# Linear-attention and token-mixer block, fp32 on one core: one transpose for the 64 leftover channels of two token tiles

## The chip, the cores and the metric

The kernel runs on one core of a Trainium2 chip. The metric is the device time of one execution in microseconds (us), lower is better. The kernel before has a median of 438.84 us over 3 runs (438.82 to 439.01).

## What is computed

x holds 2048 tokens of 448 channels. Six modulation vectors come from a condition vector; a modulated layer norm feeds a linear attention with 16 heads of 28 channels, and a second modulated layer norm feeds an MLP that mixes tokens. Everything is fp32. Cut to what matters here:

```
mod = (_silu(c) @ w_mod).reshape(c.shape[0], 6, 1, -1)
h = _layernorm(x, axis=-1) * (1 + ca) + sa
qkv = h @ wqkv
phi = lambda t: jnp.where(t > 0, t + 1, jnp.exp(t)) + 1e-6
pq, pk = phi(q), phi(k)
kv = jnp.einsum("bhsd,bhse->bhde", pk, v)
z = jnp.einsum("bhsd->bhd", pk)
o = einsum("bhqd,bhde->bhqe", pq, kv) / (einsum("bhqd,bhd->bhq", pq, z) + 1e-6)
x = x + ga * (o @ wo)
h = _layernorm(x, axis=-1) * (1 + cb) + sb
u = _gelu(jnp.einsum("bsd,sf->bdf", h, w1) + b1)
x = x + gb * (jnp.einsum("bdf,fs->bds", u, w2) + b2)
```

## The kernel before

**Numbers.** A product of fp32 matrices is made of a high and a low part of each operand (`hi` is the value rounded by a ScalarE copy, `lo` what VectorE subtracts), as hi·hi + hi·lo + lo·hi, each a TensorE matmul with a 128x128 stationary operand and up to 448 moving columns.

**Tiles.** The tokens are 16 tiles of 128. The 448 channels are contracted as three chunks of 128 and a rest of 64 (chunk 3). A tile must be transposed to bring channels onto partitions: four 128x128 TensorE transposes into the four quarters of one PSUM bank. To fill chunk 3, the 64 columns are first copied beside themselves (`a_dup`, L342, ScalarE; `b_dup`, L802, VectorE), so that after the transpose the same 64 channels stand in partitions 0–63 and 64–127. The weights of chunk 3 hold their high part in the upper 64 partitions and their low part in the lower 64. Chunk 3 then takes two matmuls (high and low part of the data) where chunks 0–2 take three each: 11 matmuls for one product.

**Order.** The program fixes each engine's order by hand: what is issued first runs first on its engine. In the profile an instruction is named by its output and inputs, such as `tp<-ident,h`.

**Phase A** (to about 105 us) goes over tiles, with tiles 0 to 2 written out. In step t of the loop over t=3..15 (L619–678) TensorE does `project` for k of tile t (`kp`, L381, 11 matmuls), the transposes of tile t+1 (`tp`, L350), and for tile t−3 `a_outer` (L478, 11 matmuls), which accumulates phi(k)ᵀh in four banks `cacc`: for each chunk high·high, low·high (phi(k)'s low part `pkl`) and, for chunks 0–2, high·low. ScalarE and VectorE split the transposed tile (`a_split`: `hh` on ScalarE L81, `hl` on VectorE L82, both 512 wide), normalise tile t+2 on VectorE (`a_norm_a` L332, `a_norm_b` L338), take exp and relu of kp (`a_exp`, ScalarE), add them to phi(k) (`pk`, VectorE L394), and split phi(k) and h. The q projections (`qp`) of most tiles come later.

**Phase B** (from about 115 us on; loop over i=0..20, L912–977) takes phi(q), already summed (`pq`), multiplies by the normalised reciprocal of the denominator (`b_scale`: `pn`, L699), duplicates the 64 columns (`b_dup`), transposes (`b_transpose`: `tq`, L809), splits (`b_high`: `pth`, ScalarE L814; `b_low`: `ptl`, VectorE L817), multiplies with the folded output weights `oh`/`ol` (`b_out`: `op`, L829, 11 matmuls), adds the residual (`b_res`: `x`, L838) and does the second layer norm in steps spread over three iterations: `b_norm1_a` (`y`, L848), `b_norm1_b` (`y`, L852, needs `rt` of the iteration before), `b_mean2` (GpSimd `ny`, ScalarE `sqb` L310), `b_norm2` (GpSimd `nb`, ScalarE `y` L870 and `h2h`), `b_low2` (`h2l`, VectorE L876). In iteration i TensorE does tq(i), op(i−1), one q projection while any are left, and from i=5 on 12 matmuls (`up`, L879–881) of the first MLP product for tile i−5. VectorE in iteration i does x(i−2), `b_prod` (`pd`, L685) for i+1, y(i−3), `b_sum` and `den` for i+1, y(i−3) again, ptl(i), pn(i+1), the duplicate of i+1, h2l(i−4), and a phi(q) sum where a q projection was made. The folded weights reach their rows by DMAs on SyncE's queue (`wp_rows`, L785–794).

The rest (both MLP products, the second by seven half-size products in the manner of Strassen) is not touched.

Of the kernel before, what the change touches and what calls it, by code (L numbers as in the profile page):

```python
# [36 lines left out]
QS = {0: 2, 4: 2}  # L37
SPLIT_AT = (8, 8, 9, 10, 11, 12, 12, 13, 13, 14, 14, 15, 15, 16, 17, 18)
# [5 lines left out]
NSLOT, NTOK = 76, 25  # L44
# [5 lines left out]
def block_kernel(ctx: ExitStack, tc: tile.TileContext, x, wqkv, wo, w1, b1, w2, b2, c, wmod, out):  # L50
# [170 lines left out]
    def w_low(j, ch):  # L221
        w, r = Whi[j, ch], raw_w[j, ch]
        if ch < 3:
            Wlo[j, ch] = moving(tslot, f"wl{j}_{ch}")
            nc.vector.tensor_sub(Wlo[j, ch], r, w.bitcast(F32))
        else:
            nc.vector.tensor_sub(w[64:128], r[64:128], w[64:128].bitcast(F32))

    def w_low_dma(j, ch):
        w, r = Whi[j, ch], raw_w[j, ch]  # L230
        if ch < 3:
            Wlo[j, ch] = moving(tslot, f"wl{j}_{ch}")
            lo, hi = Wlo[j, ch], w
        else:
            lo = hi = w[64:128]
            r = r[64:128]
        nc.scalar.activation(lo, hi.bitcast(F32), AF.Copy, scale=-1.0)
        nc.gpsimd.dma_start(lo, r, accum_op=ALU.add)
# [101 lines left out]

    def a_dup(t):
        nc.scalar.activation(hs[t][:, D:], hs[t][:, 384:D], AF.Copy)  # L342

    tps = {}

    def a_transpose(t):
        h = hs[t]
        tps[t] = bank(f"tp{t}")
        for ch in range(4):
            nc.tensor.transpose(tps[t][:, ch * P:(ch + 1) * P], h[:, ch * P:(ch + 1) * P], ident)  # L350

    def a_split(t):
        hh = slot(f"hh{t}", 512, F32R)
        hl = slot(f"hl{t}", 512, F32R)
        split(tps.pop(t), hh, hl)
        heads[t] = (hh, hl)

    def products(t, j, late):
# [3 lines left out]
        return [(hh, ch, Wlo[j, ch]) for ch in range(3)] + [(a, 3, Whi[j, 3]) for a in (hh, hl)]  # L362
# [5 lines left out]
    def project(t, j, name, late_low=False):  # L368
        hh, hl = heads[t]
        ps = bank(f"{name}{t}")  # L370
        o = ps[:, :D]
        todo = []
        for ch in range(4):
            a, b = (hh, ch, Whi[j, ch]), (hl, ch, Whi[j, ch])
            todo += [a, b] if ch == 3 else [a, (hh, ch, Wlo[j, ch]), b]
# [4 lines left out]
        for n, (a, ch, b) in enumerate(todo):  # L380
            nc.tensor.matmul(o, a[:, ch * P:(ch + 1) * P], b, start=(n == 0), stop=(n == 10))  # L381
# [87 lines left out]
    def a_outer(t):  # L469
# [4 lines left out]
        for ch in range(4):  # L474
            s = slice(ch * P, (ch + 1) * P)
            todo = [(xh, kh), (xh, kl)] + ([(xl, kh)] if ch < 3 else [])
            for i, (a, b) in enumerate(todo):
                nc.tensor.matmul(cacc[ch][:, :D], a[:, s], b, start=(t == 0 and i == 0),  # L478
                                 stop=(t == NT - 1 and i == len(todo) - 1))
# [76 lines left out]
    a_dup(1)  # L556
# [15 lines left out]
    a_dup(2)  # L572
# [13 lines left out]
    a_dup(3)  # L586
# [18 lines left out]
    a_dup(4)  # L605
# [13 lines left out]
    for t in range(3, NT):  # L619
        kp = project(t, 1, "kp")  # L620
        if t + 1 < NT:
            a_transpose(t + 1)
        a_outer(t - KV_LAG)
        if t in Q_EARLY:
# [3 lines left out]
        if t + 1 < NT:  # L628
            a_split(t + 1)
# [3 lines left out]
        for j, i in MOD_AT.get(t, ()):  # L633
            mod_part(j, i)
        if t == 14:
            fold(4)
        if 12 <= t < 16:
            nc.vector.tensor_mul(wo_sb[t - 12], wo_sb[t - 12], mods[2][:G])
        a_exp(t, kp)
        if t + 2 < NT:  # L640
            a_norm_b(t + 2)
        a_pk(t, kp)
        a_phi_q()
        a_pk_parts(t - 1)
# [138 lines left out]
    Wp_lo = [moving(tslot, f"ol{ch}") for ch in range(3)]  # L783

    def wp_rows(g, src, lows):  # L785
        r = g * G
        while r < (g + 1) * G:
            ch, at = divmod(r, P)
            n = min((g + 1) * G - r, P - at)
            if lows:  # L790
                dst = Wp_lo[ch][at:at + n] if ch < 3 else Wp_hi[3][64 + at:64 + at + n]
            else:
                dst = Wp_hi[ch][at:at + n]
# [477 lines left out]
```

## Time and profile before

| | before |
|---|---|
| median of 3 runs | 438.84 us |
| profiled execution, its own time | 439.32 us |
| span of the profile | 437.5 us |
| granted TensorE clock, mean | 0.999 |
| TensorE matmuls | busy 99% of the span, 2395 instructions |
| VectorE | busy 84%, 796 instructions |
| ScalarE | busy 62%, 576 instructions |
| GpSimd | busy 28%, 201 instructions |

The profiled execution has 1.8 us outside its span and lies 0.48 us above the median. A row of the timeline is the start in us, the duration, engine, line, operation, output and inputs with their shapes; in brackets stands how long the engine was idle before and who released it. The chain of waits is followed back from the last instruction of the program; PE is TensorE's matmul part, PEld its load of stationary operands, which runs a little ahead. On VectorE (DVE) the next instruction's start comes a little before the end of the one before it, so start-to-start distances, not durations, are what one instruction costs there.

### The profile page before, as it was taken

How to read it: one execution, taken by the hardware profiler on the slowest of the kernel's cores; microseconds unless marked ns; L12 is line 12 of the kernel's file. 1: busy time of each engine (PE TensorE's matmuls, PEld its weight loads, DVE VectorE, ACT ScalarE, POOL GpSimd, SP SyncE). 2: the span in 40 equal slices, each digit the busy share in tenths (PEclk: the TensorE clock that was granted, in tenths of full speed). 3: DMA queues.
4: the chain of work that ended last, by engine and by line, in shares of the span. 5: the costliest groups of instructions: out<-in, count | busy, mean ns of one | idle time of the engine just before them, and what ended most of it. 6: DMA issues, size and time to landing. Idle time of an engine off the chain costs nothing.

```text
span 437.5 us, 7310 instructions
## 1 busy us (share of the span) xinstructions
PE 432.9 (99%) x2395; PEld 403.1 (92%) x2395; DVE 367.0 (84%) x796; ACT 270.8 (62%) x576; POOL 123.3 (28%) x201
## 2 busy tenths in 40 slices
PE   8999999999999999999999999999999999999996
PEld 8699999999999999999999999999999999999996
DVE  5997898999898899996479487349999998898894
ACT  3768877765758877786766254235675555655550
POOL 2205676531024456664300000010112220330210
PEclk9999999999999999999999999999999999999999
DMA  8978999994422324223427446476668968877531
GB/s 229 296 221 118 173 198 228 231 237 139 144 76 50 69 52 122 50 49 81 137 78 245 163 158 185 122 195 186 154 143 188 183 141 200 177 162 208 85 49 37
DMA packets 65438, 65.18 MB, mean 149 GB/s; under 512 B 8552, under 2 KB 56952, under 8 KB 65400
## 3 DMA queue, kind: packets, MB, share of 16 engines
q1 hardware_dynamic: 54608, 47.62, 36.8%
q0 software_dynamic: 10784, 17.09, 24.5%
q8 instruction: 19, 0.31, 0.3%
q14 instruction: 19, 0.16, 0.1%
q10 hardware_dynamic: 8, 0.00, 0.0%
HBM read 41.88 MB, written 7.34 MB: 112 GB/s over the span
## 4 chain that ended last, share of the span: by engine, by line
PE 97%; DMA 1%; DVE 1%; SPq 0%; issue 0%; DVEq 0%
PE y L1087 19%; PE up L880 10%; PE up L879 10%; PE up L881 10%; PE y L1088 9%; PE op L829 8%; PE cacc L478 8%; PE qp L381 8%; PE kp L381 7%; PE tq L809 2%; PE tp L350 1%; DMA wm<-in_w_mod_dram 1%; PE kvb L752 1%; PE kp L527 1%; PE qp L527 1%; PE wp L899 1%
## 5 line engine op out<-in xcount | busy, mean ns | idle before, releaser
L880 PE MATMUL up<-h2l,ph 128*128 128x448 f32 x224 | 81.3, 363 | 0.0
L879 PE MATMUL up<-h2h,ph 128*128 128x448 f32 x224 | 81.2, 362 | 0.0
L881 PE MATMUL up<-h2h,pl 128*128 128x448 f32 x224 | 80.8, 361 | 0.0
L1047 POOL DMA_DIRECT2D a<-a x16 | 14.1, 970 | 145.8 <-DMA a<-in_B_w_dram 106.9
L879 PEld LDWEIGHTS up<-h2h,ph 128*128 128x128 f32 x224 | 42.0, 188 | 3.3
L881 PEld LDWEIGHTS up<-h2h,pl 128*128 128x128 f32 x224 | 41.9, 187 | 2.8
L880 PEld LDWEIGHTS up<-h2l,ph 128*128 128x128 f32 x224 | 42.0, 188 | 2.4
L82 DVE TENSOR_TENSOR pl<-pr,ph 128x512 fp32r<-128x512 f32 x38 | 25.9, 689 | 11.3 <-ACT ph L81 8.6
L81 ACT ACTIVATE ph<-pr 128x512 fp32r<-128x512 f32 x38 | 23.2, 621 | 17.8 <-PE up L880 11.8
L1109 ACT ACTIVATE cc<-y 128x448 f32<-128x448 f32 x24 | 13.0, 544 | 22.7 <-PE y L1088 22.7
L478 PE MATMUL cacc<-pkh,xh 128*128 128x448 f32 x64 | 24.3, 379 | 0.0
L1130 POOL DMA_DIRECT2D out_dram<-yt x14 | 14.2, 1012 | 33.7 <-DVE yt L1116 23.2
L478 PE MATMUL cacc<-pkl,xh 128*128 128x448 f32 x64 | 23.2, 362 | 0.0
L829 PE MATMUL op<-oh,pth 128*128 128x448 f32 x60 | 23.0, 383 | 0.0
L829 PE MATMUL op<-oh,ptl 128*128 128x448 f32 x60 | 21.7, 362 | 0.0
L381 PE MATMUL qp<-wh,hh 128*128 128x448 f32 x60 | 21.6, 365 | 0.0
L381 PE MATMUL qp<-wh,hl 128*128 128x448 f32 x60 | 21.4, 363 | 0.0
L381 PE MATMUL kp<-wh,hl 128*128 128x448 f32 x56 | 20.4, 364 | 0.0
L381 PE MATMUL kp<-wh,hh 128*128 128x448 f32 x56 | 20.2, 362 | 0.0
L327 POOL TENSOR_TENSOR rs<-ve,mhalf 128x1 f32<-128x1 f32 x16 | 13.9, 868 | 20.6 <-DVE ve L325 20.6
L870 ACT ACTIVATE y<-y,nb,rt 128x448 f32<-128x448 f32 x16 | 12.2, 763 | 10.7 <-POOL nb L869 10.5
L1053 DVE TENSOR_TENSOR a<-a,s 128x512 f32<-128x512 f32 (+1 forms) x32 | 18.5, 620 | 0.0
(248 smaller groups left out, 1371.6 us busy)
## 6 DMA issues: line engine op xcount, KB each, us to landing
pr<-in_B_w_dram SPq DMA_DIRECT2D x56, 256.0 KB, 3.0
a<-in_B_w_dram SPq DMA_DIRECT2D x32, 256.0 KB, 4.2
a<-in_B_w_dram SPq DMA_DIRECT2D x32, 192.0 KB, 4.6
wm<-in_w_mod_dram SPq DMA_DIRECT2D x24, 196.0 KB, 4.9
x<-in_A_x_dram SPq DMA_DIRECT2D x16, 224.0 KB, 3.8
out_dram<-x SPq DMA_DIRECT2D x14, 224.0 KB, 2.0
out_dram<-yt POOLq DMA_DIRECT2D x14, 224.0 KB, 4.6
pk<-pk POOLq DMA_DIRECT2D x12, 224.0 KB, 4.9
```

What stands on the lines that cost most here:

```text
L81: nc.scalar.activation(hi, full, AF.Copy)
L82: nc.vector.tensor_sub(lo, full, hi.bitcast(F32))
L381: nc.tensor.matmul(o, a[:, ch * P:(ch + 1) * P], b, start=(n == 0), stop=(n == 10))
L478: nc.tensor.matmul(cacc[ch][:, :D], a[:, s], b, start=(t == 0 and i == 0), stop=(t == NT - 1 and i == len(todo) - 1))
L829: nc.tensor.matmul(opb[t][:, :D], a[:, g * P:(g + 1) * P], b, start=(n == 0), stop=(n == len(todo) - 1))
L879: nc.tensor.matmul(ps[:, :D], hi[:, sl], mh, start=first, stop=False)
L880: nc.tensor.matmul(ps[:, :D], hi[:, sl], ml, start=False, stop=False)
L881: nc.tensor.matmul(ps[:, :D], lo[:, sl], mh, start=False, stop=last)
L1053: nc.vector.tensor_tensor(w, raw2[q, a][i], raw2[q, b][i], op=op)
L1087: nc.tensor.matmul(ps[:, :D], h[:, s], w, start=opens and r == r0, stop=False, skip_group_check=True)
L1088: nc.tensor.matmul(ps[:, :HD], l[:, s], wh, start=False, stop=closes and r == PAIRS - 1 - (LAST if (q, m) == (NP - 1, 6) else 0), skip_gro ...
L1130: nc.gpsimd.dma_start(of[t * P:(t + 1) * P, :], ysum.pop(t), accum_op=ALU.add)
```

## The change

From tile 6 on in phase A and tile 2 on in phase B, tiles go in pairs (6 and 7, ... 14 and 15; 2 and 3, ... 14 and 15). The second tile of a pair takes the first tile's 64 leftover columns beside its own (`a_dup`, `b_dup`, now only for second tiles), so one 128x128 transpose of chunk 3 serves both. First tiles have three transposes and no chunk 3 of their own; tiles outside pairs have three and one of 64 columns. That is 12 transposes fewer (5 in A, 7 in B).

After the transpose the 64 channels of a tile stand once, in one half of the partitions. `rem_high` (ScalarE, 64x128) rounds them in place, and `rem_low` (VectorE, 64x128) writes the low part into the other half of the partitions of the same 128x128 operand: its input and its output start 64 partitions apart. The operand of chunk 3 so holds high over low part (in the first tile of a pair low over high). The weights of chunk 3 are doubled: one tile has the high part twice, one the low part twice; the two matmuls of chunk 3 use one each. `hl` and `ptl` shrink to 384 columns, and so do the ScalarE copies to `hh` and `pth`.

```diff
+A_PAIR = 6
+B_PAIR = 2
+REM = 3 * P
-NSLOT, NTOK = 76, 25
+NSLOT, NTOK = 76, 26
     def w_low(j, ch):
         w, r = Whi[j, ch], raw_w[j, ch]
-        if ch < 3:
-            Wlo[j, ch] = moving(tslot, f"wl{j}_{ch}")
-            nc.vector.tensor_sub(Wlo[j, ch], r, w.bitcast(F32))
-        else:
-            nc.vector.tensor_sub(w[64:128], r[64:128], w[64:128].bitcast(F32))
+        Wlo[j, ch] = moving(tslot, f"wl{j}_{ch}")
+        nc.vector.tensor_sub(Wlo[j, ch], r, w.bitcast(F32))
...
     def a_dup(t):
-        nc.scalar.activation(hs[t][:, D:], hs[t][:, 384:D], AF.Copy)
+        if second(t, A_PAIR):
+            nc.scalar.activation(hs[t][:, D:], hs[t - 1][:, REM:D], AF.Copy)
+    def rem_rows(t, first):
+        up, down = slice(0, 64), slice(64, P)
+        return (down, up) if paired(t, first) and not second(t, first) else (up, down)
+    def rem_high(dst, ps, rows):
+        nc.scalar.activation(dst[rows[0], REM:], ps[rows[0], REM:], AF.Copy)
+    def rem_low(dst, ps, rows):
+        nc.vector.tensor_sub(dst[rows[1], REM:], ps[rows[0], REM:], dst[rows[0], REM:].bitcast(F32))
+    def transposes(dst, src, t, first):
+        if second(t, first):
+            nc.tensor.transpose(dst[:, REM:], src[:, REM:], ident)
+        for ch in range(3):
+            nc.tensor.transpose(dst[:, ch * P:(ch + 1) * P], src[:, ch * P:(ch + 1) * P], ident)
+        if not paired(t, first):
+            nc.tensor.transpose(dst[:64, REM:], src[:, REM:D], ident)
...
     def a_split(t):
         hh = slot(f"hh{t}", 512, F32R)
-        hl = slot(f"hl{t}", 512, F32R)
-        split(tps.pop(t), hh, hl)
+        hl = slot(f"hl{t}", REM, F32R)
         heads[t] = (hh, hl)
+        ps = tps.pop(t)
+        mine = second(t, A_PAIR) or not paired(t, A_PAIR)
+        if second(t, A_PAIR):
+            rem_high(heads[t - 1][0], ps, rem_rows(t - 1, A_PAIR))
+        nc.scalar.activation(hh[:, :REM], ps[:, :REM], AF.Copy)
+        if mine:
+            rem_high(hh, ps, rem_rows(t, A_PAIR))
+        if second(t, A_PAIR):
+            rem_low(heads[t - 1][0], ps, rem_rows(t - 1, A_PAIR))
+        nc.vector.tensor_sub(hl, ps[:, :REM], hh[:, :REM].bitcast(F32))
+        if mine:
+            rem_low(hh, ps, rem_rows(t, A_PAIR))
...
+        todo = [(ch, a, kh) for ch in range(4) for a in (xh, xl)[:1 + (ch < 3)]] + [(ch, xh, kl) for ch in range(4)]
...
     for t in range(3, NT):
-        kp = project(t, 1, "kp")
+        open_k = second(t + 1, A_PAIR)
+        kp = project(t, 1, "kp", part=0 if open_k else None)
         if t + 1 < NT:
             a_transpose(t + 1)
+            a_split(t + 1)
         a_outer(t - KV_LAG)
+        if open_k:
+            project(t, 1, "kp", part=1, o=kp)
...
+        if open_k:
+            spare()
+        if open_k:
+            if t + 2 < NT:
+                a_norm_b(t + 2)
+            a_pk_parts(t - 1)
         a_exp(t, kp)
...
     def wp_rows(g, src, lows):
...
-            if lows:
-                dst = Wp_lo[ch][at:at + n] if ch < 3 else Wp_hi[3][64 + at:64 + at + n]
-            else:
-                dst = Wp_hi[ch][at:at + n]
-            nc.sync.dma_start(dst.bitcast(F32), src[r - g * G:r - g * G + n].bitcast(F32))
+            for p0 in (at,) if ch < 3 else (at, 64 + at):
+                dst = (Wp_lo if lows else Wp_hi)[ch][p0:p0 + n]
+                nc.sync.dma_start(dst.bitcast(F32), src[r - g * G:r - g * G + n].bitcast(F32))
...
     def b_dup(t):
-        nc.vector.tensor_copy(pns[t][:, D:], pns[t][:, 384:D])
+        nc.vector.tensor_copy(pns[t][:, D:], pns[t - 1][:, REM:D])
...
+    def b_rem(t):
+        if second(t, B_PAIR):
+            rem_high(phs[t - 1][0], tps[t], rem_rows(t - 1, B_PAIR))
+            rem_low(phs[t - 1][0], tps[t], rem_rows(t - 1, B_PAIR))
+    def b_rem_own(t):
+        if second(t, B_PAIR) or t == 1:
+            rem_low(phs[t][0], rps.pop(t), rem_rows(t, B_PAIR))
...
         if i < NT:
             b_transpose(i)
+        if res:
+            b_res(i - 2)
+        if scale and i:
+            b_prod(i + 1)
+        if i < NT:
+            b_rem(i)
         if 0 <= i - 1 < NT:
             b_out(i - 1)
...
         if i < NT:
             b_high(i)
-        if res:
-            b_res(i - 2)
-        if scale and i:
-            b_prod(i + 1)
...
-        if scale:
+        if scale and second(i + 1, B_PAIR):
             b_dup(i + 1)
+        if i < NT:
+            b_rem_own(i)
         if norm2:
             b_low2(i - 4)
```

The first place is TensorE's order in phase A at step 6, tile 6 being the first of a pair. `kp6` is the k projection of tile 6, `tp7` the transpose of tile 7, `cacc` the accumulation for tile 3. Before:

```order
L381 MATMUL kp6_734<-wh1_3_268,hh6_694 128x448
L381 MATMUL kp6_734<-wh1_3_268,hl6_695 128x448
L350 MATMUL tp7_746<-ident_77,h7_698 128x128 x4
L478 MATMUL cacc0_478<-pkh3_622,xh3_543 128x448
L478 MATMUL cacc0_478<-pkl3_623,xh3_543 128x448
L478 MATMUL cacc0_478<-pkh3_622,xl3_544 128x448
```

And now, from the last product of chunk 2 on:

```order
L412 MATMUL kp6_739<-wh1_2_267,hl6_689 128x448
L359 MATMUL tp7_749<-ident_77,h7_703 128x128
L361 MATMUL tp7_749<-ident_77,h7_703 128x128 x3
L507 MATMUL cacc0_488<-pkh3_629,xh3_548 128x448
...
L507 MATMUL cacc3_491<-pkl3_630,xh3_548 128x448
L412 MATMUL kp6_739<-wh1_3_269,hh6_688 128x448
L412 MATMUL kp6_739<-wl1_3_292,hh6_688 128x448
L412 MATMUL kp7_809<-wh1_0_237,hh7_754 128x448
```

The two products of chunk 3 of tile 6 have moved behind the transposes of tile 7 and the 11 products of `a_outer`, of which the low ones (`pkl`) now stand last.

The second place is VectorE in the same step, from the phi(q) sum of tile 0 to phi(k) of tile 6. Before:

```order
L405 SCALAR_TENSOR_TENSOR pq0_732<-eq0_381,rq0_382 128x448
L82 TENSOR_TENSOR hl7_763<-tp7_746,hh7_762 128x512
L332 SCALAR_TENSOR_TENSOR h8_766<-x8_643,mv8_715,mod1_203 128x448
L338 SCALAR_TENSOR_TENSOR h8_766<-h8_766,rs8_719,mod0_285 128x448
L394 SCALAR_TENSOR_TENSOR pk6_773<-ek6_768,rk6_769 128x448
```

And now:

```order
L436 SCALAR_TENSOR_TENSOR pq0_737<-eq0_386,rq0_387 128x448
L355 TENSOR_TENSOR hh6_688<-tp7_749,hh6_688 64x128
L385 TENSOR_TENSOR hl7_755<-tp7_749,hh7_754 128x384
L355 TENSOR_TENSOR hh7_754<-tp7_749,hh7_754 64x128
L327 SCALAR_TENSOR_TENSOR h8_775<-x8_649,mv8_720,mod1_203 128x448
L333 SCALAR_TENSOR_TENSOR h8_775<-h8_775,rs8_724,mod0_286 128x448
L425 SCALAR_TENSOR_TENSOR pk6_788<-ek6_784,rk6_785 128x448
```

Two `rem_low` (L355) have come in, one ahead of the narrower `hl` and one behind it.

The third place is VectorE in one iteration of phase B, i=7, where tile 7 is the second of a pair. Before:

```order
L838 SCALAR_TENSOR_TENSOR x5_135,sm5_2173<-op5_2072,x5_135 128x448
L685 SCALAR_TENSOR_TENSOR pd8_2175<-pq8_1731,zb_1538 128x448
L848 SCALAR_TENSOR_TENSOR y4_2188<-x4_133,nm4_2109,mod4_1556 128x448
L689 TENSOR_REDUCE den8_2190<-pd8_2175 128x16
L852 SCALAR_TENSOR_TENSOR y4_2188,sy4_2192<-y4_2188,rt6_2139,mod3_1637 128x448
L817 TENSOR_TENSOR ptl7_2171<-tq7_2141,pth7_2170 128x512
L695 RECIPROCAL den8_2190<-den8_2190 128x16
L699 SCALAR_TENSOR_TENSOR pn8_2201<-pq8_1731,den8_2190 128x448
L802 COPY pn8_2201<-pn8_2201 128x64
L876 TENSOR_TENSOR h2l3_2181<-y3_2114,h2h3_2180 128x448
```

And now:

```order
L894 SCALAR_TENSOR_TENSOR x5_135,sm5_2169<-op5_2099,x5_135 128x448
L722 SCALAR_TENSOR_TENSOR pd8_2171<-pq8_1751,zb_1555 128x448
L355 TENSOR_TENSOR pth6_2123<-tq7_2164,pth6_2123 64x128
L904 SCALAR_TENSOR_TENSOR y4_2214<-x4_133,nm4_2132,mod4_1573 128x448
L726 TENSOR_REDUCE den8_2216<-pd8_2171 128x16
L908 SCALAR_TENSOR_TENSOR y4_2214,sy4_2218<-y4_2214,rt6_2162,mod3_1657 128x448
L869 TENSOR_TENSOR ptl7_2200<-tq7_2164,pth7_2199 128x384
L732 RECIPROCAL den8_2216<-den8_2216 128x16
L736 SCALAR_TENSOR_TENSOR pn8_2227<-pq8_1751,den8_2216 128x448
L355 TENSOR_TENSOR pth7_2199<-tq7_2164,pth7_2199 64x128
L932 TENSOR_TENSOR h2l3_2207<-y3_2137,h2h3_2206 128x448
```

A `rem_low` for tile 6 stands behind `pd` and reads the bank that tq(7) has just filled, and one for tile 7 stands where the duplicate of tile 8 was. In iterations whose tile is a first one neither is there, and the duplicate for the next tile stays.

More of the change, by code (lines that the diff above doesn't have):

```diff
@@ L473, in a_outer @@
         kh, kl = pks.pop(t)
[L474 to L479, printed above, removed]
+        todo = [(ch, a, kh) for ch in range(4) for a in (xh, xl)[:1 + (ch < 3)]] + [(ch, xh, kl) for ch in range(4)]
+        for i, (ch, a, b) in enumerate(todo):
+            nc.tensor.matmul(cacc[ch][:, :D], a[:, ch * P:(ch + 1) * P], b, start=(t == 0 and a is xh and b is kh),
+                             stop=(t == NT - 1 and b is kl))
     scb = {k: cst.tile([G, 64], F32, name=f"scb{k}") for k in (2, 3)}
@@ L604, in block_kernel @@
     a_norm_b(4)
-    a_dup(4)
     a_pk(1, kp1)
```

93 lines of the change are left out of this document (51 added, 42 removed).

## The prediction

> **What bounds the kernel now.** First the page: busy time by engine, and the shares of the chain that ended last.
>
> ```profile
> PE 432.9 (99%) x2395; PEld 403.1 (92%) x2395; DVE 367.0 (84%) x796; ACT 270.8 (62%) x576; POOL 123.3 (28%) x201
> ...
> PE 97%; DMA 1%; DVE 1%; SPq 0%; issue 0%; DVEq 0%
> ```
>
> TensorE is the bound nearly everywhere, so an instruction taken from it is worth its full issue time, if nothing else becomes late. The chain in order of time gives those times, phase A first, then late phase B:
>
> ```profile
> 48.10 2.21 PE kp L381 x11
> 50.31 0.44 PE tp L350 x4
> 50.75 2.21 PE cacc L478 x11
> 52.96 2.20 PE kp L381 x11
> ...
> 57.81 2.21 PE kp L381 x11
> ```
>
> ```profile
> 159.86 0.44 PE tq L809 x4
> ...
> 164.92 0.44 PE tq L809 x4
> ```
>
> A matmul of 448 columns takes 0.20 us, a transpose 0.11. An iteration of late phase B lasts 5.06 us on TensorE. The share of VectorE over the whole span, 84%, hides what matters there; its timeline in the same stretch shows it:
>
> ```profile
> 164.97 0.62 DVE L838 SCALAR_TENSOR_TENSOR x<-op,x 128x448 f32<-128x448 f32 x1
> ...
> 168.66 0.62 DVE L699 SCALAR_TENSOR_TENSOR pn<-pq,den 128x448 f32<-128x448 f32 x1
> 169.31 0.20 DVE L802 COPY pn<-pn 128x64 f32<-128x64 f32 x1
> 169.42 0.62 DVE L876 TENSOR_TENSOR h2l<-y,h2h 128x448 fp32r<-128x448 f32 x1
> 169.96 0.62 DVE L838 SCALAR_TENSOR_TENSOR x<-op,x 128x448 f32<-128x448 f32 x1
> ```
>
> From x to x it is 4.99 us without an idle moment: VectorE has 0.07 us to spare per iteration. It is a second bound right behind the first, and the change gives it work.
>
> **What TensorE gains.** 12 transposes go: 12 × 0.11 = 1.32 us. Each product keeps 11 matmuls. Early on one wait shrinks:
>
> ```profile
> 16.76 0.50 PEld L366 LDWEIGHTS kp<-wh,hl 128*128 128x128 f32 x3 [0.16 <-DVE hl L82]
> ```
>
> Here the load waits for `hl` of tile 1. That becomes 384 wide, 0.13 us shorter by the groups of VectorE, and the wait with it:
>
> ```profile
> L82 DVE TENSOR_TENSOR hl<-tp,hh 128x512 fp32r<-128x512 f32 x15 | 10.3, 686 | 2.3 <-ACT hh L81 2.2
> ...
> L437 DVE TENSOR_TENSOR xh<-h,xh 128x64 fp32r<-128x64 f32 x16 | 3.5, 220 | 2.0 <-ACT xh L433 1.9
> ...
> L426 DVE TENSOR_TENSOR xl<-h,xh 128x384 fp32r<-128x384 f32 x5 | 2.8, 553 | 0.0
> ```
>
> The six transposes that become 64 wide could save 0 to 6 × 0.055 = 0.33; the trace has none, and I take 0, since what streams through may still be 128 long. So TensorE by itself: −1.45 us.
>
> **What `rem_low` costs VectorE.** By the three groups a subtraction costs 2.1 ns a column over 220 at 64; 128 columns would last 0.29 us. How long it blocks its neighbours is another matter. The timeline has the same operation on 64 partitions that start at 64, `wh`, between two on 128:
>
> ```profile
> 18.00 1.15 DVE L225 TENSOR_TENSOR wl<-wr,wh 128x448 fp32r<-128x448 f32 x2
> 19.18 0.62 DVE L227 TENSOR_TENSOR wh<-wr,wh 64x448 fp32r<-64x448 f32 x1
> 19.84 0.63 DVE L225 TENSOR_TENSOR wl<-wr,wh 128x448 fp32r<-128x448 f32 x1
> ```
>
> The second `wl` started at 18.53 (1.15 less its own 0.62), `wh` 0.65 later and the next `wl` 0.66 after that. Where nothing changes place, a 0.62 us instruction is followed after 0.54 (pq in the next fence). So there is no overlap on either side of `wh`: 0.11 lost before it and 0.11 behind it. If `rem_low` behaves so, it costs 0.32 and another 0.12 on its predecessor: 0.44 each. If it overlaps as usual, it costs about 0.20. I take 0.44: the row differs only in that input and output there both start at 64, while in `rem_low` they start 64 apart.
>
> The Trainium skill, page "VectorE: DVE Perf Modes", section "Two Vector instructions with no wait between them", says that an instruction is held until all earlier Vector instructions have finished when an input's or the output's start quadrant (32 partitions) differs from that of the last one to read, or write, the same memory. The rows around `wh` agree (0.65 and 0.66 against 0.54), and by the rule `rem_low` is held, as is its follower: 0.44, against 0.20 without the rule. By the rule the change ends slower, without it not.
>
> **Phase A.** Rows of VectorE and of the stationary loads around steps 6 to 8:
>
> ```profile
> 51.59 0.62 DVE L405 SCALAR_TENSOR_TENSOR pq<-eq,rq 128x448 f32<-128x448 f32 x1
> 52.13 0.69 DVE L82 TENSOR_TENSOR hl<-tp,hh 128x512 fp32r<-128x512 f32 x1
> 52.73 0.68 DVE L332 SCALAR_TENSOR_TENSOR h<-x,mv,mod 128x448 f32<-128x448 f32 x1
> ...
> 56.87 0.69 DVE L82 TENSOR_TENSOR hl<-tp,hh 128x512 fp32r<-128x512 f32 x1
> ...
> 61.92 0.69 DVE L82 TENSOR_TENSOR hl<-tp,hh 128x512 fp32r<-128x512 f32 x1
> ```
>
> ```profile
> 57.85 0.19 PEld L381 LDWEIGHTS kp<-wh,hl 128*128 128x128 f32 x1
> ```
>
> After the change: pq 51.59, rem_low(6) 52.24, hl(7) 52.56, rem_low(7) 53.14, h 53.46. VectorE is 0.73 late. Meanwhile TensorE starts kp(6) at 48.10 − 0.13 − 0.11 = 47.86; after 9 products, 4 transposes and 11 products of `a_outer` it reaches the two of chunk 3 at 47.86 + 1.81 + 0.44 + 2.21 = 52.32. rem_low(6) ends at 52.53: with a load ahead of it, a stall of about 0.3. hl(8) moves to 57.60 and ends at 58.15; its load stood at 57.85 and its matmul at 57.81 + 0.40 = 58.21, so another 0.1. In step 8 rem_low(8) ends at 61.92 + 0.11 + 0.32 = 62.35 plus VectorE's lateness by then (0 to 0.6, as an earlier wait may absorb it), against a need near 62.3: 0 to 0.7, taken as 0.4. Later pairs I give nothing. Sum of stalls 0.8, bounds 0 and 1.2. Behind the waiting products stand kp(7) and all of TensorE's queue, so each stall counts fully.
>
> Saved up to tq(3): 0.13 + 6 × 0.11 = 0.79. So TensorE reaches tq(3) with a shift of −0.79 + 0.8 = 0, bounds −0.8 and +0.4.
>
> **Phase B, i=3.** Here the second tile of the first pair needs its rem_low(2) from tq(3) itself. Rows from the timeline of all engines:
>
> ```profile
> 130.43 0.60 PE L809 MATMUL tq<-ident,pn 128*128 128x128 f32 x4
> 130.56 0.68 DVE L848 SCALAR_TENSOR_TENSOR y<-x,nm,mod 128x448 f32<-128x448 f32 x1
> ...
> 132.84 0.67 ACT L310 ACTIVATE sqb<-y,ny 128x448 f32<-128x448 f32 x1 [0.52 <-POOL ny L857]
> ...
> 137.28 0.76 ACT L870 ACTIVATE y<-y,nb,rt 128x448 f32<-128x448 f32 x1 [0.76 <-POOL nb L869]
> ...
> 154.44 0.62 DVE L405 SCALAR_TENSOR_TENSOR pq<-eq,rq 128x448 f32<-128x448 f32 x1 [0.74 <-ACT rq L400]
> ```
>
> And ScalarE's groups, for `rem_high` between 254 and 292 ns (0.28):
>
> ```profile
> L814 ACT ACTIVATE pth<-tq 128x512 fp32r<-128x512 f32 x15 | 9.0, 598 | 13.5 <-PE tq L809 13.4
> ...
> L342 ACT ACTIVATE h<-h 128x64 f32<-128x64 f32 x15 | 3.8, 254 | 14.0 <-DVE h L338 14.0
> ...
> L536 ACT ACTIVATE ones_r<-ones 128x128 fp32r<-128x128 f32 x1 | 0.3, 292 | 0.0
> ```
>
> VectorE's y (L848) started at 130.56, when tq(3) had barely begun. Now it stands behind rem_low(2): the first transpose ends near 130.70, rem_high 131.02, rem_low starts at 131.06, y at 131.38. VectorE is 0.82 late, and behind the waiting instruction queue y, ptl(3) and pn(4). The chain that follows has no slack: y, then GpSimd `ny`, for which ScalarE waited 0.52, then its exp, relu and splits, GpSimd's DMA and `nb` behind those, for which ScalarE waited 0.76, and so on to the relu for which VectorE waited 0.74 at 154.44. I carry the 0.82 through to there (bounds 0 and 0.82).
>
> **Phase B, i=7 to 14.** VectorE is now continuous. Iteration of a second tile: ptl narrower −0.13; in place of the duplicate (pn to h2l took 0.76) stand pn 0.66 and rem_low 0.32, +0.22; the other rem_low +0.44: together +0.53. Iteration of a first tile: −0.13, and the duplicate no longer depends on the pn just ahead of it, −0.12: −0.25. A pair costs 2 × 4.99 + 0.28 = 10.26 us on VectorE and 2 × 5.06 − 0.11 = 10.01 on TensorE: VectorE becomes the bound. The end of this stretch:
>
> ```profile
> 194.23 0.62 DVE L699 SCALAR_TENSOR_TENSOR pn<-pq,den 128x448 f32<-128x448 f32 x1
> ```
>
> ```profile
> 194.97 0.51 PEld L809 LDWEIGHTS tq<-ident,pn 128*128 128x128 f32 x4
> ```
>
> pn(15) comes at 194.23 + 0.82 + 4 × 0.53 − 3 × 0.25 − 0.13 = 196.29; its duplicate, now needed by the first transpose of tq(15), ends 0.54 + 0.20 later, at 197.03; the load started at 194.97, so the shift is +2.1. Behind tq(15) TensorE is packed to the end of the kernel, so the shift stays.
>
> **Edits at no cost.** ScalarE has two rem_high more per pair (0.56), narrower copies and, in A, a duplicate less (0.25); the 13.4 and 14.0 us that it waits in all ahead of pth and the duplicates hide it; uncovered it would be 0.3 to 0.56 a pair. SyncE's queue gets two transfers more:
>
> ```profile
> 123.17 0.60 SPq L794 DMA_DIRECT2D oh<-wpl  x1
> ```
>
> ```profile
> ol<-wpl SPq DMA_DIRECT2D x1, 196.0 KB, 2.6
> ```
>
> ```profile
> 127.82 0.19 PEld L829 LDWEIGHTS op<-oh,ptl 128*128 128x128 f32 x1
> ```
>
> The last would be issued at 123.17 + 1.20 = 124.37 and land 2.6 later, at 126.97, before the last product of op(1); without that cover at most 0.6. Putting phi(k)'s low products last removes no wait, as the chain has none of TensorE's on them: 0.
>
> **Sum.** Profiled 439.32 + 2.1 = 441.4; less the 0.48 by which the profiled execution lies over the median: 440.9. This case's own range is 440.1 to 441.3, from the bounds of phase A (−0.8 and +0.4).
>
> **Rivals.** (1) rem_low is not held and costs 0.20. Phase A stalls 0.4, so tq(3) comes 0.4 early; VectorE is 0.3 late at i=3; second tiles then cost +0.05, first ones −0.25, and the duplicate behind pn(15) ends at 194.23 + 0.3 + 0.2 − 0.75 − 0.13 + 0.74 = 194.6, so tq(15) comes 0.4 early: 439.32 − 0.4 − 0.48 = 438.4. For it: inputs and output of `wh` are placed otherwise. Against it: the rows around `wh`. (2) The change brings what it takes off TensorE: VectorE's extra work is absorbed in its idle time (it waited 0.74 at 154.44), up to −1.45: 437.4. It decides if VectorE reaches i=7 over 1 us earlier than I carry it and rem_low costs no more than 0.20. Against: 0.07 us of slack an iteration. This is the one on the other side. (3) The stalls at chunk 3 recur in the three later pairs of phase A, 3 × 0.4: 442.1. Against: VectorE idles more there.
>
> **Chances.** Forecast 0.60 (0.03 of it within 0.2%), rival 1 0.17 (0.13 within, 0.04 faster), rival 2 0.17, rival 3 0.06. A difference of 0.2%, 0.88 us, is about what a measurement here can tell from none. Faster 0.21, same 0.16, slower 0.63. The range runs from rival 2 to just short of rival 3, 437.4 to 441.9: the two signs share the chance, so it is wide.
>
> **What would show it.** A transpose step of first tiles is 0.33 us, not 0.44. Around an L355 subtraction VectorE's starts show 0.65 ahead and 0.32 behind (held), or 0.54 and 0.20 (not). The stationary load of kp(6)'s chunk 3 waits for DVE hh. y of i=3 starts 0.8 later than before, VectorE's second-tile iterations in late B last 5.5 us, and tq's loads there wait for DVE pn. If instead TensorE's chain shows no wait for VectorE in phase B, I am wrong, and rival 1 or 2 holds.

## The result, and the profile after

The changed kernel has a median of 442.31 us over six runs (441.95 to 442.97), against 438.91 for the kernel before in six runs: ratio 1.0079, 95% interval 1.0066 to 1.0092. It is slower by 3.4 us. The forecast, 440.9, had the direction and the mechanism; it was 1.4 us short, and the measured time lies 0.4 us beyond the upper end of the range.

The page after: TensorE has lost its hold on the chain that ended last, and VectorE has taken a sixth of it.

```profile
PE 432.6 (98%) x2383; PEld 399.5 (91%) x2383; DVE 372.0 (85%) x818; ACT 271.3 (62%) x596; POOL 122.2 (28%) x201
...
PE 73%; DVE 16%; ACT 5%; issue 3%; POOL 1%; DVEq 0%; ACTq 0%; POOLq 0%
```

The total hides it again: VectorE went from 84% to 85%. Where the chain leaves TensorE says more. Here are pieces of it in order of time, first from before (the first k product of tile 0), then from after:

```profile
12.91 1.50 PE kp L527 x4
```

```profile
12.20 1.50 PE kp L556 x4
...
42.53 0.55 ACT eq L430
...
84.26 0.55 PE tp L361 x3
...
128.15 2.21 PE qp L412 x11
131.46 0.69 DVE y L904
...
138.18 0.77 ACT y L926
...
198.28 2.21 PE op L885 x11
```

Three things are to be read here. The profiled execution of before started its products 0.71 us later than that of after, behind a load of `wm`, so differences below are counted from there: add 0.71 to after minus before. From y (L904) at 131.46, the instruction that the prediction named at i=3, up to tq(15) the chain no longer runs through TensorE but through VectorE, ScalarE and GpSimd. And it leaves TensorE in phase A too: from 42.53 to 84.26 all of it is VectorE, ScalarE, GpSimd and gaps between them, up to the transposes of tile 14.

VectorE's timeline over one iteration with a second tile (i=7) and one with a first tile (i=8):

```profile
155.90 0.62 DVE L894 SCALAR_TENSOR_TENSOR x<-op,x 128x448 f32<-128x448 f32 x1
...
156.44 0.62 DVE L722 SCALAR_TENSOR_TENSOR pd<-pq,zb 128x448 f32<-128x448 f32 x1
157.09 0.29 DVE L355 TENSOR_TENSOR pth<-tq,pth 64x128 fp32r<-64x128 f32 x1
157.42 0.69 DVE L904 SCALAR_TENSOR_TENSOR y<-x,nm,mod 128x448 f32<-128x448 f32 x1
...
158.55 0.68 DVE L908 SCALAR_TENSOR_TENSOR y<-y,rt,mod 128x448 f32<-128x448 f32 x1
...
159.27 0.56 DVE L869 TENSOR_TENSOR ptl<-tq,pth 128x384 fp32r<-128x384 f32 x1
...
160.02 0.62 DVE L736 SCALAR_TENSOR_TENSOR pn<-pq,den 128x448 f32<-128x448 f32 x1
160.67 0.28 DVE L355 TENSOR_TENSOR pth<-tq,pth 64x128 fp32r<-64x128 f32 x1
160.99 0.62 DVE L932 TENSOR_TENSOR h2l<-y,h2h 128x448 fp32r<-128x448 f32 x1
161.53 0.61 DVE L894 SCALAR_TENSOR_TENSOR x<-op,x 128x448 f32<-128x448 f32 x1
...
163.74 0.67 DVE L908 SCALAR_TENSOR_TENSOR y<-y,rt,mod 128x448 f32<-128x448 f32 x1
...
164.34 0.55 DVE L869 TENSOR_TENSOR ptl<-tq,pth 128x384 fp32r<-128x384 f32 x1
...
166.26 0.62 DVE L894 SCALAR_TENSOR_TENSOR x<-op,x 128x448 f32<-128x448 f32 x1
```

rem_low is held as forecast: 0.65 from pd to it and from pn to it, 0.33 and 0.32 to what follows. One cost is new: ptl comes 0.72 after y (L908) in the second tile's iteration and 0.60 after it in the first tile's. The iterations take 5.63 and 4.73 us, a pair 10.36, against TensorE's 10.0.

### The profile page after: what moved, and what is told of

Read it like the earlier page. It is cut to its first block, busy times and chain, and to the rows that moved or that the text cites. A ratio compares the mean times of both kernels' runs of the same rounds, so it can differ in the third digit from the quotient of the medians.

```text
span 439.9 us, 7361 instructions
## 1 busy us (share of the span) xinstructions
PE 432.6 (98%) x2383; PEld 399.5 (91%) x2383; DVE 372.0 (85%) x818; ACT 271.3 (62%) x596; POOL 122.2 (28%) x201
## 4 chain that ended last, share of the span: by engine, by line
PE 73%; DVE 16%; ACT 5%; issue 3%; POOL 1%; DVEq 0%; ACTq 0%; POOLq 0%
PE y L1147 19%; PE y L1148 9%; PE up L936 8%; PE up L935 8%; PE up L937 8%; PE qp L412 6%; PE cacc L507 4%; PE kp L412 3%; PE op L885 2%; DVE y L904 1%; DVE y L908 1%; DVE h L327 1%; DVE x L894 1%; DVE pd L722 1%; DVE h L333 1%
## 5 line engine op out<-in xcount | busy, mean ns | idle before, releaser
L1190 POOL DMA_DIRECT2D out_dram<-yt x14 | 12.7, 906 | 36.4 <-DVE yt L1176 27.0
L885 PE MATMUL op<-ol,pth 128*128 128x448 f32 x60 | 21.7, 362 | 0.0
L412 PE MATMUL qp<-wl,hh 128*128 128x448 f32 x60 | 21.4, 363 | 0.0
L412 PE MATMUL kp<-wl,hh 128*128 128x448 f32 x56 | 20.3, 363 | 0.0
L1064 DVE TENSOR_TENSOR u<-u,mod 128x448 f32<-128x448 f32 x14 | 8.7, 621 | 11.3 <-ACT u L1063 11.0
```

What stands on the lines that cost most here:

```text
L885: nc.tensor.matmul(opb[t][:, :D], a[:, g * P:(g + 1) * P], b, start=(n == 0), stop=(n == len(todo) - 1))
```

## The experiments

Each is given with the median of the kernel before, measured beside it; "over" and "under" mean against that median. Of an edit only the telling lines are shown, and `...` marks what is left out.

**Phase A alone, phase B alone.** In the first, phase B is that of the kernel before; in the second, phase A is (with the new order of `a_outer`).

```diff
+        nc.vector.tensor_sub(phs[t][1], tps.pop(t)[:P if t else G, :], phs[t][0].bitcast(F32))
...
-            b_rem(i)
...
-        if scale and second(i + 1, B_PAIR):
+        if scale:
             b_dup(i + 1)
...
-            b_rem_own(i)
```

> Only phase A is changed (pairs from tile 6 on, weights of q and k doubled, the new order of its loop); phase B is as before. Theory: in the trace of the changed kernel TensorE reaches phase B 0.6 us late although five transposes and a shorter wait save it 0.68, so phase A stalls it by about 1.2 us; behind that phase B runs with its old 0.07 us of slack on VectorE and nothing is added. 438.9 + 0.6 = 439.5. Rival (the cost lies in phase B alone, what phase A shows is paid back there): the saving of 0.7 shows, 438.2.

Measured 439.96 against 439.06: 0.9 over, ratio 1.0021 (1.0012 to 1.0030).

```diff
-        transposes(tps[t], h, t, A_PAIR)
+        for ch in range(4):
+            nc.tensor.transpose(tps[t][:, ch * P:(ch + 1) * P], h[:, ch * P:(ch + 1) * P], ident)
```

> Only phase B is changed (and the order of the products of a_outer); phase A splits and projects as before. Theory: TensorE reaches tq(3) 0.11 early; VectorE is 1.13 late there against TensorE (it waits for all four transposes, then for ScalarE, then does the held subtraction), each of four second tiles costs it 0.64 more and each first one 0.25 less: -0.11 + 1.13 + 4 x 0.64 - 3 x 0.25 - 0.13 = 1.7 at pn(15), and with the duplicate that tq(15) now needs first (0.74 behind pn, where it had 0.0 spare) 2.4 to 2.7: 441.3 to 441.6. Rival (a subtraction costs only its instruction, 0.20, held or not): VectorE stays below TensorE's 10.0 us a pair, 438.1 to 438.6. Rival (whichever phase delays VectorE first sets the end, the two do not add): as the whole change, 442.3.

Measured 441.78 against 439.06: 2.7 over, ratio 1.0062 (1.0049 to 1.0074). Both parts lose, as the theory had it, and the losses add to 3.6, about the whole. The rival that phase A's loss is paid back in phase B falls.

**No change of partitions.** The same instructions in the same order, but on all 128 partitions in place.

```diff
+    def rem_low_all(dst, ps):
+        nc.vector.tensor_sub(dst[:, REM:], ps[:, REM:], dst[:, REM:].bitcast(F32))
...
-            rem_low(heads[t - 1][0], ps, rem_rows(t - 1, A_PAIR))
+            rem_low_all(heads[t - 1][0], ps)
...
-            rem_low(phs[t - 1][0], tps[t], rem_rows(t - 1, B_PAIR))
+            rem_low_all(phs[t - 1][0], tps[t])
```

> The whole change, but in pairs rem_high and rem_low work on all 128 partitions in place, so that no VectorE instruction changes its partitions. The number of instructions, their columns, their order and their waits are the same; chunk 3 of a paired tile then holds low parts only, which leaves its high part out of the products. Theory (the hold is what costs): starts around each of these subtractions go from 0.65 and 0.33 to 0.54 and 0.20, ptl's 0.72 back to 0.47 plus what precedes it as usual, a second tile costs VectorE 0.05 more instead of 0.64, a pair takes it less than TensorE's 10.0 us: 438.3 to 439.2. Rival (the number of instructions and their waits on ScalarE cost it, the partitions do not matter): within 0.6 us of the whole change, 441.7 or more.

Measured 439.74 against 439.06: 0.7 over, ratio 1.0018 (1.0009 to 1.0027). The whole change lay at 442.35 beside it, so 2.6 us of its loss go with the partitions, at an equal number of instructions. Its VectorE in i=7:

```profile
154.78 0.62 DVE L908 SCALAR_TENSOR_TENSOR x<-op,x 128x448 f32<-128x448 f32 x1
...
155.32 0.62 DVE L732 SCALAR_TENSOR_TENSOR pd<-pq,zb 128x448 f32<-128x448 f32 x1
155.86 0.28 DVE L358 TENSOR_TENSOR pth<-tq,pth 128x128 fp32r<-128x128 f32 x1
156.06 0.68 DVE L918 SCALAR_TENSOR_TENSOR y<-x,nm,mod 128x448 f32<-128x448 f32 x1
...
157.18 0.68 DVE L922 SCALAR_TENSOR_TENSOR y<-y,rt,mod 128x448 f32<-128x448 f32 x1
...
157.78 0.55 DVE L881 TENSOR_TENSOR ptl<-tq,pth 128x384 fp32r<-128x384 f32 x1
...
159.80 0.62 DVE L908 SCALAR_TENSOR_TENSOR x<-op,x 128x448 f32<-128x448 f32 x1
```

The subtraction now starts 0.54 behind pd and is followed after 0.20, ptl 0.60 after y, and the iteration takes 5.02 us. This is the experiment that decides for the hold. That these subtractions also cover 128 partitions and not 64 is not what frees them: in the whole change the second rem_low (160.67) is on 64 partitions too but reads PSUM from partition 0, and the next reader of PSUM, x at 161.53, comes the usual 0.54 after its neighbour. The time came out above the range of the theory (439.2): the early wait is still in it, as the tenth experiment shows.

**The changed kernel once more.**

> The changed kernel once more, for its spread (441.95 to 442.97 in six runs, where the kernel before spreads by 0.26) and for a second profile. If VectorE and what it waits for bind it through phases A and B, its stalls of TensorE in phase A differ from run to run by some tenths and the tq loads of phase B from tile 8 on wait for VectorE in every run: 442.3 with a spread of about 1 us. Rival (the spread is in the loads at the start alone): the times from tq(0) to the end agree within 0.1 us between the two profiles.

Measured 442.35 (442.17 to 442.61), ratio 1.0075 (1.0062 to 1.0089). Of this loss 0.2 us lie outside the span, 1.9 to 2.0 us here against 1.7 to 1.8 before, for a reason that no run shows. Counted from the first k product, the two profiles agree within 0.05 us at tq(0), at tq(15) and at the last product, so for these two the rival holds: what differed lay ahead. Between kernels with the same phase A it does not hold (below, with the two reorderings).

**Two orders.** In the whole change rem_low of a first tile stands early, so that y and, on TensorE, the products of chunk 3 stand behind it. In this experiment it is moved back:

```diff
+            b_out(i - 1, 0 if second(i, B_PAIR) else None)
...
             b_norm1_b(i - 3, i)
+        if i < NT:
+            b_rem_low(i)
...
             b_rem_own(i)
+            if second(i, B_PAIR):
+                b_out(i - 1, 1)
```

> The whole change, but in phase B the first tile's rem_low stands behind the second y (L908 of the change) on VectorE, and the two chunk-3 products of a first tile's op stand behind the MLP's products on TensorE, so that neither waits for it. The hold stays, and so does VectorE's 10.36 us a pair. Theory: the wait at i=3, 1.13 us, is carried to the end as one term of the sum; without it 442.3 - 1.1 = 441.2, up to 441.6 if x of a first tile now waits for its later products. Rival (VectorE's throughput alone sets the end, an early wait is made up): 442.0 to 442.4.

Measured 440.73 against 439.2: 1.5 over, ratio 1.0040 (1.0028 to 1.0053), so 1.5 to 1.7 less than the whole change by the ratios (1.0075 and 1.0079), and below the range that was expected. The rival falls: the early wait is a term of its own. But the edit does more than take it away, since VectorE's pair no longer takes 10.36 us. In i=7:

```profile
155.75 0.62 DVE L899 SCALAR_TENSOR_TENSOR x<-op,x 128x448 f32<-128x448 f32 x1
...
158.67 0.29 DVE L355 TENSOR_TENSOR pth<-tq,pth 64x128 fp32r<-64x128 f32 x1
159.00 0.56 DVE L872 TENSOR_TENSOR ptl<-tq,pth 128x384 fp32r<-128x384 f32 x1
...
161.26 0.62 DVE L899 SCALAR_TENSOR_TENSOR x<-op,x 128x448 f32<-128x448 f32 x1
```

ptl now stands right behind rem_low, so one hold does for what were two, and the iteration takes 5.51 us, not 5.63. Over four second tiles that is 0.5 us. The rest is the early wait: counted from the first k product, x of i=7 starts 0.7 us later than before, where in the whole change it was 1.6.

In the whole change the early wait is seen twice: in TensorE's load for op(6), and in what stands behind tq(3), whose first load is the row at 129.99:

```profile
129.99 0.14 PEld L359 LDWEIGHTS tq<-ident,pn 128*128 128x128 f32 x1
...
157.44 0.19 PEld L885 LDWEIGHTS op<-oh,pth 128*128 128x128 f32 x1 [1.21 <-DVE pth L355]
```

```profile
130.83 0.27 ACT L352 ACTIVATE pth<-tq 64x128 fp32r<-64x128 f32 x1 [1.45 <-PE tq L361]
```

```profile
131.13 0.29 DVE L355 TENSOR_TENSOR pth<-tq,pth 64x128 fp32r<-64x128 f32 x1 [1.02 <-ACT pth L352]
131.46 0.69 DVE L904 SCALAR_TENSOR_TENSOR y<-x,nm,mod 128x448 f32<-128x448 f32 x1
```

The other order is in phase A alone: the second half of the normalisation ahead of spare work.

```diff
         if open_k:
-            spare()
-        if open_k:
             if t + 2 < NT:
                 a_norm_b(t + 2)
+            spare()
```

> Only phase A is changed, as in the first experiment, and in the steps whose tile opens a pair the second half of the next normalisation stands ahead of the spare work on VectorE (modulation sums, scaling of wo) and not behind it. In the first experiment TensorE stood still for 0.63 us ahead of the transposes of tile 14, which waited for that half. Theory (that one place in the order costs it): 439.96 - 0.6 = 439.3. Rival (VectorE is late in any case, and the stall moves to the next thing that it makes): 439.8 to 440.1.

Measured 439.57 against 439.2: 0.4 over, ratio 1.0009 (1.0000 to 1.0018), beside 1.0021 (1.0012 to 1.0030) without it. The intervals overlap: inconclusive by itself. So both orders were tried together on the whole change:

> The whole change with the fifth and the sixth experiment's orders together (normalisation ahead of spare work in phase A; a first tile's rem_low behind the second y, its chunk-3 products behind the MLP's). The held subtractions stay. Theory (the terms add): 442.3 - 1.6 - 0.5 = 440.2, what is left over the kernel before being the held subtractions' share of VectorE's 10.3 us a pair. Rival (each edit relieves the same wait): 440.7 or more.

Measured 441.28 against 438.99, ratio 1.0052 (1.0039 to 1.0064), no better than the sixth alone. The theory falls for phase A: the stall ahead of tile 14's transposes is gone from the trace, and others stand in its place.

```profile
62.99 0.19 PEld L412 LDWEIGHTS kp<-wh,hh 128*128 128x128 f32 x1 [0.49 <-DVE hh L355]
...
88.72 0.19 PEld L412 LDWEIGHTS kp<-wh,hl 128*128 128x128 f32 x1 [0.64 <-DVE hl L385]
```

VectorE is late in phase A, and which of its products TensorE then waits for differs from one profile to the next: with the same phase A, the fifth experiment's profile reached tq(0) 0.5 us late and this one 1.4, and the whole change 0.6 and the first experiment 1.1. What makes the difference is open.

**What is left without both.** The third and the sixth experiment together:

> The third and the sixth experiment together: rem_high and rem_low of pairs on all 128 partitions in place (chunk 3 of a paired tile then holds low parts only), rem_low of a first tile behind the second y on VectorE, the chunk-3 products of its op behind the MLP's. Theory (hold and early wait are the whole loss; what is left is the kernel with 12 transposes fewer): the time of the kernel with nothing in their place, 0.2 us under the kernel before, at most 0.2 over it. Rival (the added instructions or transfers cost something of their own): 0.5 us or more over it, as in the third experiment.

Measured 438.33 against 439.15: 0.8 under, ratio 0.9982 (0.9974 to 0.9991). That is better than its theory had it, which allowed 0.2 under. Hold and early wait are the whole loss; without them a saving shows, and the chain is TensorE's again:

```profile
PE 97%; DMA 1%; DVE 1%; SPq 0%; issue 0%; ACT 0%; DVEq 0%
```

In this profile TensorE's last product comes 1.1 us earlier than before, counted from the first k product. Of the 1.45 us that the prediction gave TensorE by itself, 0.45 are lost in one wait:

```profile
158.84 0.31 PEld L367 LDWEIGHTS tq<-ident,pn 128*128 128x128 f32 x3 [0.45 <-ACT sqb L305]
```

**The saving by itself.** The transposes left out of the kernel before, with nothing put in their place.

```diff
-        for ch in range(4):
+        for ch in range(3 if lone(t, 6) else 4):
...
-        for g in range(4):
+        for g in range(3 if lone(t, 2) else 4):
```

> The kernel before, without the 12 chunk-3 transposes of the tiles that would be first of a pair, their duplicates and the last 128 columns of their splits, and with nothing put in their place: their products of chunk 3 use chunk 2's columns, which leaves those 64 channels out. Theory (TensorE is the bound, a transpose costs its 0.11 us of issue): 438.9 - 1.3 = 437.6. Rival (transposes run beside matmuls, or something else binds at once): 438.3 to 438.9.

Measured 439.03 against 439.2, ratio 0.9993 (0.9983 to 1.0003): no difference in time that can be measured, so the theory falls. But a part of each execution's time lies outside its span. In the kernel before that part was 1.7 to 1.8 us in all 22 executions; here it was 2.2 to 2.8 in five of 12, for a reason that no run shows. The spans alone are 0.6 us shorter than before (mean 436.85 against 437.47, 95% interval 0.1 to 1.1), near the 0.8 of the tenth experiment. So a part of the saving is there.

In the profile, which is of an execution with a span of 437.3, TensorE reaches tq(15) 0.9 us ahead and then waits in the last iterations, where VectorE has modulation sums (`acc`, L185) besides:

```profile
193.95 0.42 PEld L817 LDWEIGHTS tq<-ident,pn 128*128 128x128 f32 x4 [0.54 <-issue]
...
201.77 0.19 PEld L212 LDWEIGHTS modp<-ml,ones_r 112*128 112x128 f32 x1 [0.47 <-DVE ml L82]
...
206.48 0.19 PEld L889 LDWEIGHTS up<-h2h,ph 128*128 128x128 f32 x1 [0.39 <-DVE x L848]
```

So these sums were moved forward, in that kernel and, as a control, in the kernel before:

```diff
-        if i == NT - 4:
+        if i == 0:
             load_mod(5)
-        if NT - 3 <= i < NT:
-            mod_part(5, i - NT + 3)
+        if i in (4, 5):
+            mod_part(5, 2 * (i - 4))
+            mod_part(5, 2 * (i - 4) + 1)
```

> The seventh experiment's kernel (12 transposes less, nothing in their place, 64 channels of the first tiles left out), and the four modulation sums that VectorE makes in iterations 13 to 16 of phase B stand in iterations 4 and 5, with their loads earlier. Theory (the saving got lost there, because VectorE, which has 0.07 us to spare an iteration, gets 0.6 us more in each of these): TensorE's waits at tq(15), at the modulation's matmuls and at the MLP's products behind them go, and 0.9 to 1.3 us under the kernel before are left. Rival (the end of the layer norm's chain binds there anyway): 0.2 to 0.4 under it.

> The kernel before with the modulation sums moved in the same way, nothing else: the control of the one before. Theory: TensorE hardly waited there, so within 0.2 us of the kernel before. Rival (the sums cost TensorE time in the kernel before too): 0.5 us or more under it.

Measured 440.11 (ratio 1.0020, 1.0010 to 1.0031) and 440.39 (1.0029, 1.0020 to 1.0039) against 439.15. Neither theory held. In the control the spans are 1.0 us longer than before. In the eleventh they are those of the kernel before (median 437.35 against 437.45), and it is again the part outside, 1.9 to 3.8 us, that makes the time longer; against the seventh its median span has grown by 0.6. The waits of the last iterations are gone from the eleventh's trace; in both a new one stands at tq(8), 1.42 and 1.44 us long. In the control:

```profile
160.55 0.42 PEld L809 LDWEIGHTS tq<-ident,pn 128*128 128x128 f32 x4 [1.44 <-ACT sqb L310]
```

Work put on VectorE at i=4 and 5 came back as a wait three iterations later, as the wait at i=3 did in the change: the chain there has too little slack for it in the kernel before too. The tenth experiment leaves the sums in their place and its profile has no such wait in the last iterations; why is open. The two profiles are no fair pair, though: the seventh's span is above the median of its kernel (436.75), the tenth's, 436.2, below (436.6).

**One edit alone.** phi(k)'s low products last, in the kernel before:

> The kernel before with one edit of the change alone: in a_outer phi(k)'s low products stand last. TensorE waited for none of them before, so the theory expects the time of the kernel before within 0.2 us. Rival (the order matters by itself): 0.4 us or more either way.

Measured 439.36 against 439.15, ratio 1.0001 (0.9992 to 1.0009): no difference, as expected.

**Another way without a hold.** Low parts of both tiles by one wide subtraction, high parts doubled by ScalarE, weights in both orders:

```diff
+    def twin_first(dst, ps):
+        for rows in (slice(0, 64), slice(64, P)):
+            nc.scalar.activation(dst[rows, REM:], ps[64:, REM:], AF.Copy)
+    def twin_own(dst, ps):
+        nc.scalar.activation(dst[64:, REM:], ps[:64, REM:], AF.Copy)
...
+        todo += [(hh, 3, Whi[j, 3]), (zs3[t], 3, Wr[j]) if t in zs3 else (hl, 3, Whi[j, 3])]
```

> The same 12 transposes fewer in another way: VectorE subtracts the second tile's whole 512 columns in one instruction as before, so that one 128x128 tile holds both tiles' low parts, each in its half; ScalarE copies the high parts so that they stand in both halves (three copies of 64x128 a pair), and the low parts meet weights in the order high over low for the second tile and low over high for the first (what the other tile's half adds is a low part times a low part). No VectorE instruction is added or changes partitions; the first tile's two products of chunk 3 stand behind a_outer in phase A and behind the MLP's products in phase B. Theory (VectorE's held instructions and its wait at i=3 are what turned the change around): VectorE needs less than before, TensorE's saving remains, 437.5 to 438.0. Rival (ScalarE's added copies, 0.8 us a pair, delay the layer norm in the iterations where the chain through ScalarE has no slack): 438.6 or more.

Measured 447.41 against 439.2, ratio 1.0187 (1.0173 to 1.0200). ScalarE and VectorE waited for each other at the same bank; first ScalarE, then VectorE:

```profile
63.02 0.56 ACT L359 ACTIVATE hh<-tp 64x128 fp32r<-64x128 f32 x2 [1.73 <-DVE hl L85]
```

```profile
171.86 0.69 DVE L883 TENSOR_TENSOR ptl<-tq,pth 128x512 fp32r<-128x512 f32 x1 [1.59 <-ACT pth L359]
```

With ScalarE's copies ahead of the wide one, and the fifth experiment's order of the normalisation:

> The eighth experiment's kernel with its ScalarE copies in another place. There the trace shows each copy out of a transposed bank waiting until VectorE was through with its subtraction from that bank (1.73 us at tile 9 in phase A), and in phase B VectorE's ptl waiting for the copies (1.59 us). Now the two copies for the first tile stand ahead of the second tile's wide copy, and the third behind sqb (in phase A behind exp and relu); the normalisation also stands ahead of the spare work as in the fifth experiment. Theory (it was the order of ScalarE's copies; VectorE has no held instruction and one instruction a pair less than in the tenth experiment): 438.0 to 438.6, under the kernel before. Rival (ScalarE's three copies a pair are too much in themselves): 440 or more.

Measured 441.52 against 438.99, ratio 1.0062 (1.0048 to 1.0075). The orders were 6 us of the 8. What is left is as the rival had it, though no run takes ScalarE's copies apart from the rest. In late phase B the chain now runs between ScalarE and GpSimd, and a pair takes 10.6 us on them:

```profile
165.97 1.05 POOL rt L941
...
167.31 0.77 ACT y L947
...
168.11 0.58 ACT h2h L950
168.69 0.65 ACT sqa L313 x2
169.34 0.65 ACT sqb L313 x2
...
172.01 0.94 POOL pl L285
```

No version here that computes the whole result beats the kernel before.

## Why the prediction was short

**The mechanism held, step by step.** rem_low is held, 0.65 and 0.33 against 0.65 and 0.32; VectorE becomes the bound from i=7 on; a first tile's iteration costs 0.26 less (0.25); the wait at i=3 is carried unchanged, 1.6 us at y there and 1.6 at x of i=7 (0.91 and 0.71). tq(15) starts 2.65 + 0.71 = 3.4 late (before, at 194.97), and 3.2 of it are left at the last product of the kernel:

```profile
197.62 0.14 PEld L359 LDWEIGHTS tq<-ident,pn 128*128 128x128 f32 x1 [0.99 <-issue]
```

So the direction was no luck.

**What failed is the size of three terms of the sum.**
- "Sum of stalls 0.8" in phase A, TensorE at tq(3) with a shift of 0. Measured there: 129.99 − 130.22 + 0.71 = +0.5, just beyond the bound of 0.4. With the 0.79 saved, the stalls were 1.3 us and not 0.8. The first was put at kp(6), with 0.3; in this profile VectorE was there in time, while in that of the first experiment the stall stands there, with 0.28. Here they come at kp(8) (0.32), at `hl` of tile 10 (0.16) and above all ahead of tile 14's transposes (0.85):

```profile
61.24 0.19 PEld L412 LDWEIGHTS kp<-wh,hh 128*128 128x128 f32 x1 [0.32 <-DVE hh L355]
```

```profile
84.25 0.31 PEld L361 LDWEIGHTS tp<-ident,h 128*128 128x128 f32 x3 [0.85 <-DVE h L333]
```

"Later pairs I give nothing" was the error: the prediction followed VectorE's lateness up to step 8 only, but the chain stays off TensorE up to tile 14.
- "VectorE is 0.82 late" at i=3. Against TensorE it was 1.1: I let rem_high start when chunk 3's transpose had ended; by the row above it started when all four had, 0.84 after the first load. The Trainium skill, page "PSUM — Partial Sum Buffer", section "Terms", says that two engines must not use the same bank and quadrant at once, reads included. The trace agrees with a program that keeps them apart bank by bank (rem_high behind all four transposes here, ScalarE behind VectorE for 1.73 us in the eighth experiment).
- "+0.53" for a second tile. Measured 5.63 − 4.99 = 0.64: ptl is held too, 0.72 against 0.60 after y, though three instructions stand between it and rem_low. ptl is the first to read PSUM after a rem_low that read it from partition 64. I had looked only at the instruction next to it, and the `wh` rows, from which the 0.44 came, read no PSUM. The third experiment agrees: 0.60 there. The Trainium skill, page "VectorE: DVE Perf Modes", section "Two Vector instructions with no wait between them", judges PSUM and SBUF apart, by the last instruction that read each. The trace agrees with it (0.72 against 0.60).

With the measured sizes the same sum is 0.5 + 1.1 + 4 × 0.64 − 3 × 0.26 − 0.13 = 3.3. One reading was wrong without harm: VectorE's three groups give 1.04 ns a column, not 2.1. The 0.29 us for rem_low follows from 1.04 and is what the rows show.

**The range.** The forecast's own, 440.1 to 441.3, held the bounds of phase A alone. The wait at i=3 had bounds of 0 and 0.82 with the estimate at the upper one, and the second tiles had none, so nothing let these two terms grow. The lower end stood on rival 2 with its −1.45 us; the most that a run here gained is 0.8 (1.1 at the end of its interval), in the tenth experiment, which leaves out part of the result.

**The chances.** Rivals 1 and 2 fell with the rows of rem_low, rival 3 was half right: stalls in later pairs of phase A (tiles 10 and 14), though not at chunk 3. The low products last at zero stand by the ninth experiment. The two SyncE transfers at zero were not tried alone; the tenth experiment keeps them and still gains. The 64-wide transposes at zero stand by this piece of the chain after, 0.11 as for a full one:

```profile
14.04 0.11 PE tp L363
```

## What to carry to other kernels

Before work is taken from the engine that is the bound, look at what the next one has to spare in that very stage: here 0.6 us more in every second iteration, where 0.07 were free, and little more room in phase A, turned 1.3 us of saved transposes into a loss of 3.4. Price an instruction by its distances to its neighbours, and where it reads from other partitions than the rest, look also at the next one that reads the same memory, here three instructions on. A wait that is put into a chain with little slack comes back far behind (from i=3 at x of i=7, from i=4 and 5 at tq(8)): look for it where the chain ends, not where it was put. And before a small time is called nothing, see whether it lies in the span of the work or outside it.

## What the runs showed of the hardware

- A VectorE subtraction of 128 columns costs 0.20 us between neighbours that start at the same partition (third experiment) and 0.44 where it reads at one half and writes at the other (the change). Where it reads PSUM from partition 64, another 0.12 falls on the next reader of PSUM, three instructions later.
- A transpose of 64 columns takes TensorE the same 0.11 us as one of 128.
- In these programs ScalarE, VectorE and TensorE take turns at one PSUM bank, even for different columns of it: waits of up to 1.73 us in the eighth experiment. What the chip would do without these waits no run shows.
